# Loading chunk 4's K ahead of three weight pieces, and chunk 2's V beside chunk 3's, in a delta-rule attention and SwiGLU kernel

## The chip, the cores and the metric

The kernel runs on one core of one Trainium2 chip. The metric is the device time of one execution in microseconds; the times given are the median, the lowest and the highest of the runs.

## The reference

The input is `q`, `k`, `v` of shape (4, 8, 768, 48), `beta` of shape (4, 8, 768), all float32, and three weight matrices of a feed-forward block, which arrive as 64-bit floats. An attention without softmax (the delta rule) walks over the 768 positions with one 48 x 48 state for each of the 4 x 8 heads; its output, as 3072 tokens of 384 features, goes through a SwiGLU block:

```python
k_n = k / (np.linalg.norm(k, axis=-1, keepdims=True) + 1e-06)
for t in range(S):
    kt, vt, bt = (k_n[:, :, t], v[:, :, t], beta[:, :, t, None])
    y[:, :, t] = np.einsum('bhd,bhde->bhe', q[:, :, t], state)
    v_old = np.einsum('bhde,bhd->bhe', state, kt)
    state = state + bt[:, :, :, None] * np.einsum('bhd,bhe->bhde', kt, vt - v_old)
x = y.transpose(0, 2, 1, 3).reshape(B * S, H * D)      # (3072, 384)
g = x @ w_gate                                         # (384, 1536)
out = (g * (1.0 / (1.0 + np.exp(-g))) * (x @ w_val)) @ w_out   # w_out (1536, 384)
```

## The kernel before

The 768 positions are cut into 12 chunks of 64. In a chunk the recurrence becomes matrix products: a triangular matrix from the products of K with itself is inverted (for pairs of chunks at once, by substitution), and the state is carried from chunk to chunk. `advance(c)` is a generator that does chunk c's part of the recurrence in steps, so that its small matmuls can be put between the large ones of the feed-forward block of the chunk before. For each chunk, K, Q and V are loaded from DRAM by `load_k(c)`, `load_q(c)` (two DMAs of 192 KB each, in runs of 48 numbers, 192 bytes) and `load_v(c)` (four of 96 KB, in the same runs). `turned(c, of_q)` transposes K or Q on TensorE through the identity (L511), and ScalarE copies the result out of PSUM (L515). K's buffers: chunk 4 uses that of chunk 0 again, and so its load stands in `advance(0)` behind the products that read chunk 0's K last (`of_state`, L1145). V has two buffers, which chunks 2 and 3 take over from chunks 0 and 1.

The weights come in 42 pieces, numbered from 0: 24 of 128 x 256 numbers for features 0 to 1023 (gate and value by turns), 6 of 128 x 512 for the rest, and 12 of the output matrix. A piece is read as it is, two 32-bit words for each weight, into a place that is free at the moment (`stage`, L260: its DMA's queue is SyncE's). ScalarE (`power_step`, L272 and L278) and then VectorE (`convert`, L289, L297, L309) turn the pairs of words into 32-bit weights. The first 23 pieces are staged by hand-written calls. A `stage(n, after)` of these puts a one-element copy on GpSimd ahead of the DMA (L259), which reads a piece `after` that was staged 2 or 3 earlier, and so keeps the DMA back until that piece has landed. The pieces from 23 on are staged by `convert`, when it has freed the place that they take (`freed_by`).

The order on each engine is the order of the program: the whole body stands under a manual schedule. All the loads named here are issued by SyncE, one after the other; a load that waits holds up what stands behind it on that queue, and of the DMAs that it issued at most 8 are on their way at a time, since the ninth takes the semaphore of the first.

The stage around the change is the first 130 us. `chain(at)` runs inside the first two feed-forward groups (chunk 0, f = 0 and 2), four times in each, and advances chunk 0 and then chunk 1 by a step each time. Then follow, for chunks 0 and 1, the groups `(c, f)` in the order (0,4), (0,6), (1,0), (1,2), (1,4), (1,6), (0,8), (1,8), (0,10), (1,10) of `gate_val` (L1409): twelve matmuls each for gate and value, a silu on ScalarE (L1418), a product on VectorE (L1420), and conversions of the next pieces in between (`fill`). Gate and value products go through four PSUM banks by turns, so a group uses the banks of the group two before it. Between groups, `point(2)` puts in a step of preparation: first `turned(4, False)` with `turned(2, True)`, which need K(4) and Q(2), then their products (L527); later the same for K(5). `small_unread(40)`, which stands ahead of `turned(4, False)`, issues tiny matmuls (L658). Behind all groups follow the output products of chunks 0 and 1 (L1436), with the preparation of chunk 2 between them, and from chunk 2 on another form of the feed-forward block (L1313, L1519).

As the kernel stands, the queue of SyncE in this stretch is: pieces 18 to 22, Q(2), V(2), K(4), piece 23, piece 29, V(3), piece 24, K(5), pieces 25, 26, 28, 27.

Of the kernel before, what the change touches and what calls it, by code (L numbers as in the profile page):

```python
# [20 lines left out]
def kernel(  # L21
# [75 lines left out]
    QB = 2  # L97
# [37 lines left out]
    def halves(x, c, b):  # L135
        return x[NB * b : NB * b + NB, :, c * C : (c + 1) * C, :]

    def load_heads(t, x, c, dmas=(nc.sync,)):
        for b in range(2):
            dmas[b % len(dmas)].dma_start(  # L140
                out=t[64 * b : 64 * b + 64, :, :, 0:D].rearrange(
                    "p bp h d -> p (bp h) d"
                ),
                in_=halves(x, c, b).rearrange("bp h p d -> p (bp h) d"),
            )

    def load_k(c, dmas=(nc.sync,)):
        load_heads(kn_of(c), k, c, dmas)

    def load_q(c):  # L150
        load_heads(qpad[c % QB], q, c)
# [28 lines left out]
    def load_v(c):  # L180
        vin[c] = work.tile([128, 2, NB, NJ, D], FP32, name="vin", bufs=2)
        for b in range(2):
            src = halves(v, c, b).rearrange("bp (j par) p d -> par p (bp j) d", par=2)
            for par in range(2):
                s = 64 * (b ^ par)
                nc.sync.dma_start(
                    out=vin[c][s : s + 64, par].rearrange("p bp j d -> p (bp j) d"),
                    in_=src[par],
                )
# [22 lines left out]
    def words(tile_):  # L212
        return tile_.bitcast(U32)
# [32 lines left out]
    def stage(n, after=None, queue=nc.sync):  # L246
        _, src, t, f0, m = pieces[n]
        name, lo = place_of[n]
        if name not in places:
            if name == "p_sb":  # L250
                places[name] = words(p_places[0])
            else:
                places[name] = work.tile(
                    [128, 2 * PIECE], U32, name="staged", tag=name, bufs=1
                )
        place = places[name][:, lo : lo + 2 * m]
        staged[n] = place
        if after is not None:
            nc.gpsimd.tensor_copy(place[:, 0:1], staged[after][:, 0:1])  # L259
        queue.dma_start(  # L260
            out=place, in_=src[t * 128 : (t + 1) * 128, f0 : f0 + m].bitcast(U32)
        )
# [104 lines left out]
    def new_n(g):  # L367

        n_t[g] = work.tile([128, 2, HH], FP32, name="n_t")
# [58 lines left out]
    def load_beta():  # L428
        for s_ in range(2):
            for par in range(2):  # L430
                at = beta_rows(s_).start + 8 * par
                nc.gpsimd.dma_start(
                    out=beta_s[at : at + 8],
                    in_=beta.rearrange(
                        "(b bp) (j par) s -> b par (bp j) s", b=2, par=2
                    )[s_ ^ par, par],
                )
# [123 lines left out]
    def gram(*args):  # L561
        for _ in gram_steps(*args):
            pass
# [384 lines left out]
    def advance(c):  # L948
# [170 lines left out]
                    if n + par < 3:  # L1119
                        yield MORE  # L1120
        if c + 2 < NCH:
            if c < 2:
                load_v(c + 2)
            else:
                late_loads.append(lambda: load_v(c + 2))
        yield
        pq = p_sb.pop(c)
# [489 lines left out]
    def converts(n):  # L1617
        if todo:
            convert(todo[:n])
            del todo[:n]  # L1620
# [9 lines left out]
    def step(kind, fn, *args):  # L1630
        key = (kind, args or (1,))
        if key not in gens:
            gens[key] = [fn(*args), 0]
        if next(gens[key][0], None) != MORE:
            gens[key][1] += 1

    def steps(kind, *args):
        return gens.get((kind, args), (None, 0))[1]
# [123 lines left out]
    with tc.manual_schedule(  # L1762
        engines={
            mybir.EngineType.PE,
            mybir.EngineType.Activation,
            mybir.EngineType.DVE,
            mybir.EngineType.SP,
            mybir.EngineType.Pool,
        }
    ):  # L1770
        new_n(0)
        load_beta()
        first_tiles()
        norms(0)
        norms(1)
        load_q(0)
        load_k(2)
        load_k(3)
        load_q(1)
        load_v(0)  # L1780
        copy_a = nc.scalar.copy
        small_unread(48)
        unread(2)
        turned(0, False, 0)
        p_g = [first_gram(0, "px")]
        turned(1, False, 2)
        first_diag(0, p_g[0])
        spread_beta(copy_a)
        p_g.append(first_gram(1, 2))
        r_b = first_n()  # L1790
        first_diag(1, p_g[1])
        nc.vector.transpose(first_of["mb"][:, 0 : R * R], first_of["flat"])
        first_scale(r_b)
        for n in range(12):
            stage(n, n - 2 if n > 1 else None)
            if n == 9:
                load_v(1)
        stage(12, 10)
        stage(13, 11)
        unread(2, "py")  # L1800
        small_unread(16, "py")
        low_copies(0, p_g[0])
        turned(0, True, 0)
        low_copies(1, p_g[1])
        turned(2, False, "py")
        turned(3, False, "px")
        first_q = [gram_steps(0, True, 2)]
        next(first_q[0])
        turned(1, True, 0)
        gram(2, False, "py", (copy_a, copy_a))  # L1810
        gram(3, False, "px", (copy_a, copy_a))
        unread(2, 0)
        first_q.append(gram_steps(1, True, 0))
        next(first_q[1])
        power_step(0)
        first_substitution()
        for n in range(14, 18):
            stage(n, n - 3)
        first_z()
        some, others = slice(0, HH // 2), slice(HH // 2, HH)  # L1820
        spread_z(0, 1, nc.scalar, some)
        for n in range(18, 23):
            stage(n, n - 3)
        load_q(QB)
        spread_z(0, 0, nc.vector)
        spread_z(0, 1, nc.vector, others)
        scale_v(0)
        next(first_q[0])
        new_nt(0, qpad[1].rearrange("p bp h d -> p (bp h d)"))
        zb_1 = work.tile([128, R, R], FP32, name="zb", bufs=1)  # L1830
        new_nt(1, zb_1.rearrange("p k i -> p (k i)"))
        step("advance", advance, 0)
        next(first_q[1])
        for x in range(2):
            spread_z(1, x, nc.scalar)
        for n in (2, 4, 1, 3, 5, 6, 7):
            power_step(n)
        for _ in range(6):
            step("advance", advance, 0)
        converts_first(0)  # L1840
        step("advance", advance, 0)
        converts_first(2)
        p_n = banks("p_n", "px")
        n_products(1, p_n, (0,))
        step("advance", advance, 0)
        converts_first(4)
        n_products(1, p_n, (1,))
        converts_first(1, 3)
        converts_first(5)
        scale_v(1)  # L1850
        n_copies_1(p_n, zb_1.rearrange("p k i -> p (k i)"))

        def chain(at):

            step("advance", advance, 0 if steps("advance", 0) < 4 else 1)
            converts((1, 2, 2, 1)[at])

        pairs = [(c, f) for c in range(2) for f in range(0, 8, 2)]
        pairs += [(c, f) for f in range(8, FT, 2) for c in range(2)]
        for at, (c, f) in enumerate(pairs):  # L1860
            early = c == 0 and f < 4
            if c == 1 and f == 0:
                finish(1)
                second_inverse.append(invert(1))
                for _ in range(3):
                    next(second_inverse[0])
            elif not early:
                point(2)
            need((6, 12, 18, 24, 30, 30)[f // 2])
            gate_val(c, f, fill, at, chain if early else None)  # L1870
        need(len(pieces))
        for bp in range(NB):
            point(2)
            output(0, bp, fill, (4, 8))
        output(1, 0, fill, (4, 8))
        hold.clear()
        first_blocks(True)
        first_blocks(False)
        point(2)
        output(1, 1, fill, range(2, FT, 2))  # L1880
        finish(2)
        x_sums(2)
        sums_of_w(12)
        for c in range(2, NCH):
            if c > FAST:
                begin(c, 0)
            point(c + 1)
            if c == FAST:
                begin(c, 0)
            for r in range(ROUNDS):  # L1890
                gate_val_fast(c, r, fill)
            output_fast(c, fill)
            finish(c + 1)
            x_sums(c + 1)
# [30 lines left out]
```

## Time and profile before

| | |
|---|---|
| median of 3 runs | 693.07 us (692.01 to 694.98) |
| profiled execution: time | 694.12 us |
| profiled execution: span from first to last instruction | 692.4 us |
| TensorE busy | 675.3 us, 98% |
| VectorE, ScalarE, GpSimd busy | 414.2, 262.9, 193.1 us |
| mean granted clock of TensorE | 0.995 |
| read from and written to DRAM | 53.58 MB, 7.08 MB |

In the lines of the profile PE is TensorE's matmuls, PEld its weight loads, DVE VectorE, ACT ScalarE, POOL GpSimd and SPq the queue of SyncE, from which DMAs are issued. L511 is line 511 of the kernel. A row of a timeline has the start in us, the length in us, the engine, the line, the operation, what is written from what, and how many; in brackets stands the idle time of the engine before it and what ended that. Tiles are named without their numbers, so `kn` is K of any chunk, `zt`, `wo_sb`, `p_sb` and `staged` are places in which pieces are staged, and `ffn` is any of the four banks.

### The profile page before, as it was taken

Reading aid. Unit: us, or ns where it says so; the run is one execution under the profiler, and the core shown is the slowest. Engines: PE = TensorE matmul, PEld = TensorE weight load, DVE = VectorE, ACT = ScalarE, POOL = GpSimd, SP = SyncE. Lnnn points to the kernel's source line nnn. Section 1 sums busy time; section 2 is a strip of 40 time slices with the busy share of each in tenths; the row PEclk is TensorE's granted clock in tenths of the full one; section 3 lists DMA queues with packets and bytes.
Section 4 is the critical chain, followed back from the end, with each engine's and each line's share of the span. In section 5 each row is a group of like instructions: output and inputs, shape, how many; then the busy total and the mean of one; then the engine's idle time right before and its main releaser. Section 6 shows DMA issues by size and latency. Waiting matters only on the chain.

```text
span 692.4 us, 24603 instructions
## 1 busy us (share of the span) xinstructions
PE 675.3 (98%) x10836; PEld 630.0 (91%) x10836; DVE 414.2 (60%) x874; ACT 262.9 (38%) x557; POOL 193.1 (28%) x310
## 2 busy tenths in 40 slices
PE   8897999999999999999999999999999999999997
PEld 4786888756999999999999999999999999999997
DVE  7898489798666765647456546655555534433342
ACT  4785576213543533344323245232143242142230
POOL 5110031105893037820037830208810000000000
PEclk9999899999999999999999999999999999999999
DMA  9667925007561621464333364243243221221210
GB/s 133 160 177 180 257 69 161 1 24 163 134 121 25 114 81 40 97 113 93 78 87 71 70 128 81 55 97 83 55 109 69 56 63 47 55 62 46 70 46 24
DMA packets 143850, 62.24 MB, mean 90 GB/s; under 512 B 122976, under 2 KB 126048, under 8 KB 143744
## 3 DMA queue, kind: packets, MB, share of 16 engines
q1 hardware_dynamic: 141536, 60.19, 37.6%
q8 instruction: 85, 1.39, 0.9%
q10 hardware_dynamic: 2080, 0.39, 0.4%
q14 instruction: 21, 0.17, 0.1%
q0 software_dynamic: 128, 0.10, 0.1%
HBM read 53.58 MB, written 7.08 MB: 88 GB/s over the span
## 4 chain that ended last, share of the span: by engine, by line
PE 91%; DVE 3%; ACT 2%; DMA 2%; issue 1%; SPq 0%; DVEq 0%; ACTq 0%
PE ffn L1313 42%; PE ffn L1519 20%; PE ffn L1409 9%; PE ffn L1436 4%; DMA kn<-in_k_dram 2%; PE p_px L977 2%; PE p_py L960 2%; PE p_px L1043 2%; PE p_py L1133 2%; PE p_px L1145 1%; PE p_px L527 1%; PE p_py L1206 1%; PE ffn L1072 1%; PE p_px L921 1%; PE p_py L935 1%
## 5 line engine op out<-in xcount | busy, mean ns | idle before, releaser
L1313 PE MATMUL ffn<-x_ffn,wg_sb 128*128 128x128 f32 x840 | 128.5, 276 | 0.5 <-ACT ffn L1369 0.3
L1313 PE MATMUL ffn<-x_ffn,wv_sb 128*128 128x128 f32 x840 | 128.2, 275 | 0.0
L1313 PEld LDWEIGHTS ffn<-x_ffn,wg_sb 128*128 128x128 f32 x840 | 111.1, 192 | 1.0 <-ACT ffn L1369 0.7
L1313 PEld LDWEIGHTS ffn<-x_ffn,wv_sb 128*128 128x128 f32 x840 | 110.7, 192 | 0.0
L1348 DVE TENSOR_TENSOR h_f<-sil,ffn 128x256 f32<-128x256 f32 x120 | 49.7, 418 | 83.2 <-ACT sil L1343 81.8
L1343 ACT ACTIVATE sil<-ffn 128x256 f32<-128x256 f32 x120 | 45.8, 383 | 128.5 <-PE ffn L1313 126.4
L1519 PE MATMUL ffn<-wo_sb,h_f 128*128 128x192 f32 x480 | 83.4, 328 | 0.0
L860 POOL TENSOR_TENSOR n_b<-mb,half 128x32 f32<-128x32 f32 x5 | 30.0, 6006 | 183.6 <-DVE mb L569 183.6
L1519 PEld LDWEIGHTS ffn<-wo_sb,h_f 128*128 128x128 f32 x480 | 78.1, 190 | 0.3
L599 POOL TENSOR_TENSOR tmp<-zb,mb 128x31 f32<-128x31 f32 (+15 forms) x124 | 68.6, 553 | 16.9 <-DVE mb L586 7.5
L605 POOL TENSOR_TENSOR zb<-zb,tmp 128x31 f32<-128x31 f32 (+15 forms) x124 | 70.0, 565 | 9.7
L1480 DVE TENSOR_TENSOR ffn<-ffn,p_sb 128x512 f32<-128x512 f32 x58 | 40.4, 696 | 49.1 <-ACT ffn L1369 47.7
L1313 PE MATMUL ffn<-x_t,h_f 128*128 128x128 f32 x480 | 61.0, 280 | 0.2 <-ACT ffn L1326 0.2
L1313 PEld LDWEIGHTS ffn<-x_t,h_f 128*128 128x128 f32 x480 | 56.3, 192 | 2.1 <-ACT ffn L1326 0.3
L1480 DVE TENSOR_TENSOR o_sb<-o_sb,ffn 128x192 f32<-128x192 f32 x49 | 17.2, 352 | 64.1 <-PE ffn L1519 61.5
L1326 ACT COPY ffn<-ffn 128x512 f32<-128x512 f32 x30 | 17.1, 571 | 60.8 <-PE ffn L1313 60.8
L1477 DVE TENSOR_TENSOR h_f<-h_f,h_f 128x256 f32<-128x256 f32 x60 | 29.4, 493 | 11.8 <-PE ffn L1519 10.5
L1519 PE MATMUL ffn<-last_k,h_f 128*128 128x192 f32 x200 | 36.0, 327 | 0.0
L1409 PE MATMUL ffn<-x_ffn,wg_sb 128*128 128x256 f32 x144 | 34.4, 385 | 0.3 <-DVE x_ffn L1210 0.3
L1409 PE MATMUL ffn<-x_ffn,wv_sb 128*128 128x256 f32 x144 | 33.8, 382 | 0.0
L1519 PEld LDWEIGHTS ffn<-last_k,h_f 128*128 128x128 f32 x200 | 32.9, 190 | 0.1
L1409 PEld LDWEIGHTS ffn<-x_ffn,wg_sb 128*128 128x128 f32 x144 | 26.7, 191 | 4.6 <-DVE wg_sb L309 0.8
(323 smaller groups left out, 1123.9 us busy)
## 6 DMA issues: line engine op xcount, KB each, us to landing
h_f<-w_s SPq DMA_DIRECT2D x60, 256.0 KB, 2.8
p_sb<-w_s SPq DMA_DIRECT2D x27, 256.0 KB, 2.8
vin<-in_v_dram SPq DMA_DIRECT2D x48, 96.0 KB, 3.4
out_dram<-o_sb SPq DMA_DIRECT2D x48, 96.0 KB, 2.2
kn<-in_k_dram SPq DMA_DIRECT2D x20, 192.0 KB, 4.6
zt<-in_moe_w_out_dram SPq DMA_DIRECT2D x6, 384.0 KB, 3.9
qpad<-in_q_dram SPq DMA_DIRECT2D x36, 64.0 KB, 3.3
w_s<-h_f SPq DMA_DIRECT2D x7, 256.0 KB, 3.5
```

The lines of the kernel that those rows point to most:

```text
L599: engine.tensor_tensor(out=t_v, in0=zb[:, 0 : j + 1, j : j + 1].to_broadcast([128, j + 1, m]), in1=mb[:, j : j + 1, j + 1 : R].to_broadcas ...
L605: engine.tensor_tensor(out=zb[:, 0 : j + 1, j + 1 : R], in0=zb[:, 0 : j + 1, j + 1 : R], in1=t_v, op=ALU.add,)
L860: nc.gpsimd.tensor_tensor(out=n, in0=mb.rearrange("p j i -> p (j i)")[:, 0 : R * R : R + 1], in1=half, op=ALU.pow,)
L1313: nc.tensor.matmul(p[:, u], w(u), moving, start=start and u == 0, stop=True, skip_group_check=True,)
L1326: nc.scalar.copy(p_y, p_x)
L1343: nc.scalar.activation(sil[:, n].rearrange("p (i n) -> p i n", i=2), p[:, 0:2], ACTF.Silu)
L1348: nc.vector.tensor_tensor(out=h_of(c, f, j), in0=sil[:, n].rearrange("p (i n) -> p i n", i=2), in1=p[:, 2:4], op=ALU.mult,)
L1409: nc.tensor.matmul(ps[name][:, i], w_sb[:, t, (f + i) * 128 : (f + i + 1) * 128], xts[c][:, t], start=(t == 0 and i == 0), stop=(t == KT - 1),
L1436: nc.tensor.matmul(p_o, hs[c, f - f % 2][:, f % 2, bp * 128 : (bp + 1) * 128], wo_sb[:, f], start=(f == 0), stop=(f == FT - 1),)
L1477: nc.vector.tensor_tensor(out=out, in0=a, in1=b, op=ALU.subtract)
L1480: nc.vector.tensor_tensor(out=out, in0=a, in1=b, op=ALU.add)
L1519: nc.tensor.matmul(p[x, part], a(f - f % 2)[:, f % 2], b(f), start=not begun and f == 0, stop=f == FH - 1, skip_group_check=True,)
```

## The change

`load_v(2)`, which stood at the end of `advance(0)`'s correction steps, moves into `advance(1)`, directly ahead of `load_v(3)`. Of the hand-staged pieces, 20, 21 and 22 and then `load_q(2)` move from ahead of the first products of chunk 0 into `chain`, behind the step of chunk 0 that issues `load_k(4)`. SyncE's queue thereby becomes: pieces 18, 19, K(4), pieces 20, 21, 22, Q(2), piece 23, piece 29, V(2), V(3), piece 24, K(5), pieces 25, 26, 28, 27. The instructions of TensorE, VectorE, ScalarE and GpSimd and their order stay as they are; only the semaphores that some of them wait on are other ones.

```diff
         if c + 2 < NCH:
-            if c < 2:
-                load_v(c + 2)
-            else:
+            if c == 1:
+                load_v(2)
+                load_v(3)
+            elif c > 1:
                 late_loads.append(lambda: load_v(c + 2))
...
-        for n in range(18, 23):
+        for n in range(18, 20):
             stage(n, n - 3)
-        load_q(QB)
         spread_z(0, 0, nc.vector)
...
+        later_pieces = list(range(20, 23))
+
         def chain(at):
 
             step("advance", advance, 0 if steps("advance", 0) < 4 else 1)
+            if later_pieces:
+                for n in later_pieces:
+                    stage(n, n - 3)
+                later_pieces.clear()
+                load_q(QB)
             converts((1, 2, 2, 1)[at])
```

## The prediction

> **What bounds the kernel now.** I read the chain of waits first, because TensorE is busy for nearly the whole span and only the chain says where the rest sits. In order of time (start us, length us, what), around the changed place:
>
> ```profile
> 64.18 6.36 DMA kn<-in_k_dram
> ...
> 70.67 1.94 PE p_px L511 x8
> 72.62 1.64 PE p_py L511 x8
> 74.25 5.18 PE ffn L1409 x24
> ...
> 82.56 35.66 PE ffn L1409 x164
> 118.23 0.87 PE p_px L511 x8
> ```
>
> From 55 us to 124 us the chain is TensorE, except for one 6.36 us piece: the load of chunk 4's K, which `turned(4, False)` (L511) transposes. The timeline of TensorE gives the idle time itself, and the windows of 52 to 76 us (us; PE, PEld, DVE, ACT, POOL busy; granted clock; DMA share; GB/s) give clock and transfers:
>
> ```profile
> 65.00 0.70 PE L658 MATMUL p_px<-half 32*32 32x1 f32 x64 [0.19 <-issue]
> 70.67 1.94 PE L511 MATMUL p_px<-ident,kn 128*128 128x128 f32 x8 [4.97 <-DMA kn<-in_k_dram]
> ```
> ```profile
> 52.00:58.00 6.00, 6.00 (x200) 4.90 (x194) 4.22 (x9) 3.88 (x11) 0.68 (x5) 1.00 0.50 163
> 58.00:64.00 6.00, 5.87 (x199) 4.82 (x192) 5.50 (x15) 3.40 (x9) 0.00 (x0) 1.00 0.88 184
> ...
> 66.00:68.00 2.00, 0.00 (x0) 0.00 (x0) 1.90 (x7) 0.00 (x0) 0.00 (x0) 0.81 0.79 179
> 68.00:74.00 6.00, 3.33 (x16) 3.36 (x17) 0.81 (x3) 1.83 (x4) 0.00 (x0) 0.50 0.79 176
> ...
> 80.00:82.00 2.00, 2.00 (x103) 1.88 (x96) 2.00 (x8) 1.46 (x3) 0.00 (x0) 1.00 1.00 406
> ```
>
> So the stall costs twice. TensorE stands from 65.70 to 70.67 us, **4.97 us**, and the granted clock falls to 0.50, so the 16 transposes behind it take 1.94 + 1.64 = 3.58 us. Eight of them take 0.87 us at full clock (118.23), so 2 x 0.87 = 1.74 us would do: another **1.84 us**. Together **6.81 us**. The transfer engines were only half busy from 52 to 58 us, before K was issued.
>
> **Part 1: K(4) goes ahead of pieces 20 to 22.** SyncE's queue as it is now, and the marker copy on GpSimd that releases piece 21:
>
> ```profile
> 52.47 0.38 SPq L260 DMA_DIRECT2D wo_sb<-in_moe_w_val_dram  x1
> 52.94 0.38 SPq L260 DMA_DIRECT2D zt<-in_moe_w_gate_dram  x1
> 56.19 0.33 SPq L260 DMA_DIRECT2D zt<-in_moe_w_val_dram  x1
> 56.83 1.34 SPq L260 DMA_DIRECT2D zt<-in_moe_w_gate_dram  x1
> 58.25 1.32 SPq L140 DMA_DIRECT2D qpad<-in_q_dram  x2
> 59.68 2.97 SPq L186 DMA_DIRECT2D vin<-in_v_dram  x4
> 62.77 2.24 SPq L140 DMA_DIRECT2D kn<-in_k_dram  x2
> 65.13 0.64 SPq L260 DMA_DIRECT2D zt<-in_moe_w_val_dram  x1
> ...
> 66.64 3.69 SPq L186 DMA_DIRECT2D vin<-in_v_dram  x4
> ...
> 74.95 1.63 SPq L260 DMA_DIRECT2D wo_sb<-in_moe_w_val_dram  x1
> ```
> ```profile
> 55.98 0.18 POOL L259 COPY zt<-wo_sb 128x1 uint32<-128x1 uint32 x1 [3.35 <-DMA wo_sb<-in_moe_w_gate_dram]
> ```
>
> Rows for K's issues (ns min/median/max) and its landing, then Q's landing, then V's issues:
>
> ```profile
> L140 SPq DMA_DIRECT2D kn<-in_k_dram x4: 596/748/1370, 62.8 to 74.2; - x4
> ...
> DMA to landing us min/median/max: 4.2/4.8/6.4
> ```
> ```profile
> DMA to landing us min/median/max: 3.8/4.8/5.7
> ```
> ```profile
> L186 SPq DMA_DIRECT2D vin<-in_v_dram x12: 606/633/1505, 36.2 to 69.7; - x12
> ```
>
> Piece 19 is issued at 52.47, 20 at 52.94. In the new program order K's two issues stand between them. K's buffer is free by then: its last readers, chunk 0's 64 L1145 matmuls, stand much earlier in the program. At worst its issues take 1.37 us each, so the second starts at 54.3 and lands 6.4 us later, at 60.7; at best 53.6 + 4.2 = 57.8. TensorE asks at 65.70, so at least 5.0 us of room remain, and the 4.97 us go.
>
> What K pushes: piece 20 from 52.94 to between 54.1 and 55.7. Piece 21 waits for GpSimd's copy (55.98), which waits for piece 18's landing, and piece 18 stays ahead of K, so 21 and 22 keep 56.19 and 56.83. The three copies keep their order on GpSimd, where nothing stands between them and the earlier ones. Cost: nothing, covered by SyncE's 2.87 us of waiting between 53.32 and 56.19; without that cover it would be K's 2.24 us on everything behind.
>
> **Part 2: what is late next.** Q(2) stays at about 58.25, its second half starting near 58.9; 5.7 us later is 64.6. The L511 transposes of it are reached at 65.70 + 0.87 = 66.57, so 2 us remain. Piece 23 no longer stands behind V(2) and K(4). That matters, for ScalarE's rows are:
>
> ```profile
> 71.74 0.43 ACT L272 ACTIVATE wv_sb<-zt 128x256 f32<-128x256 f32 x1 [5.95 <-DMA zt<-in_moe_w_val_dram]
> ...
> 80.54 0.71 ACT L272 ACTIVATE wv_sb<-wo_sb 128x512 f32<-128x512 f32 x1 [1.94 <-DMA wo_sb<-in_moe_w_val_dram]
> ...
> 88.49 3.94 ACT L856 COPY a_sb<-a_sb 32x1024 f32<-32x1024 f32 x2
> ```
>
> ScalarE is in order: today it waits for piece 23 until 71.74, with the copies of K's transposes behind that. Behind Q(2) piece 23 is issued near 59.6, 5.5 us earlier, and so is there near 66.2, 0.4 us after ScalarE begins to wait for it (71.74 - 5.95 = 65.79); the copies behind it are needed by matmuls that come after the next 5.18 us group (74.25), so that costs nothing. V(2) and V(3) aren't urgent: `scale_v(2)` and `advance(2)` stand behind the output of chunks 0 and 1.
>
> **Part 3: the weights behind V.** Here most of the gain could be lost. TensorE comes 6.81 us earlier, but piece 25 (74.95 issue, 80.54 on ScalarE) comes earlier only by what the queue sheds. Everything from 58.25 to 74.95 stays in the stretch, except K's issues: from 62.77 to 65.13, **2.36 us**. V(2) and V(3) keep their eight issues (2.97 + 3.69 us). Bounds: 0 if the transfers rather than the issues set the time and half-used time was not gained, 2.36 if the rows carry over. I take 2.36, since SyncE issued nearly without a break in this stretch.
>
> From 80.54 ScalarE works through its list nearly without a gap to the end of L856 at 92.43, which VectorE waits for. The consequences meet TensorE at the value matmuls of chunk 1, f = 4, whose bank VectorE must have read:
>
> ```profile
> 92.46 2.25 DVE L569 STREAM_TRANSPOSE mb<-a_sb 128x512 f32<-128x512 f32 x2 [2.73 <-ACT a_sb L856]
> ...
> 96.36 0.68 DVE L1420 TENSOR_TENSOR h_f<-sil,ffn 128x512 f32<-128x512 f32 x1
> ```
> ```profile
> 99.93 2.75 PE L1409 MATMUL ffn<-x_ffn,wv_sb 128*128 128x256 f32 x12
> ```
> ```profile
> 130.86 0.69 DVE L1420 TENSOR_TENSOR last_h<-sil,ffn 128x512 f32<-128x512 f32 x1 [3.09 <-PE ffn L1409]
> ```
>
> VectorE is done with that bank at 96.36 + 0.68 = 97.04; TensorE comes at 99.93: slack 2.89 us. TensorE 6.81 us earlier and VectorE 2.36 us earlier leaves a new wait of 6.81 - 2.36 - 2.89 = **1.56 us**. Later VectorE waits 3.09 us for TensorE (130.86), more than the 2.89 us by which it can now trail; from there both go on together, so nothing more is lost.
>
> **Sum.** 6.81 - 1.56 = **5.25 us**. The profiled execution's span of 692.4 becomes 687.2 us, its time of 694.12 us becomes 688.9; the median of the runs shown is 1.05 us lower, 693.07, and 5.25 off that is **687.8 us**.
>
> [...]
>
> **The rivals.**
>
> *All of the lead is kept.* If SyncE sheds more than K's issues (the transfers used the idle half of 52 to 58 us as well, or V's issues get shorter with less ahead of them), the wait at L1409 vanishes: 6.81 us, **686.3 us**. For it: SyncE's 3.69 us for four V issues against 4 x 0.63 = 2.5 us at the median. Against: 3.9 us must be shed.
>
> *The queue sheds little.* If bytes set the time, K's two halves of 192 KB at the 406 GB/s of the 80 to 82 us window are 0.97 us: gain 0.97 + 2.89 = 3.86 us, **689.2 us**; with nothing shed, 2.89 us and 690.2. Against: 163 to 184 GB/s in the stretch, far from 406. [...]
>
> *The new wait drops the clock.* The window of 66 to 68 us has a mean clock of 0.81, so 0.76 us at half: it fell at 67.24, 1.54 us after TensorE's last matmul. A wait of 1.56 us is as long. Then 1.84 us go again: gain 3.41, **689.7 us**. Against: ahead of the old drop stood more than a microsecond of tiny 32x1 matmuls, ahead of the new wait full ones. [...]
>
> *The change doesn't do what it says.* Q(2) becomes the late one and replaces K's wait; to undo all it would have to land 6 us later than now, near 70.5: **693.1 us**.
>
> *Slower: eight V issues in a row hold the weights back.* If each takes the longest row, 1.505 us, the two V loads take 12.04 instead of 6.66 us, and piece 25 comes 5.38 - 2.36 = 3.02 us later than now. The wait at L1409 is then 6.81 + 3.02 - 2.89 = 6.94 us and halves the clock: 6.81 - 6.94 - 1.84 = -1.97, **695.0 us**. It decides once ScalarE gets piece 25 later than 81.6 us (1.05 us later than now). For it: V's issues did stretch behind K. Against: the loads ahead of them are the same ones less K.
>
> **How the numbers follow.** Forecast 0.58, all the lead kept 0.14, little shed 0.10, clock drop 0.08, Q late 0.05, slower 0.05. A measurement of this kernel can tell 0.5%, 3.5 us, from no change. Faster by more: forecast, all kept, 0.06 of little shed, 0.04 of the clock drop, 0.82. Slower by more: 0.03, where the V loads hold more than priced. The rest, 0.15, is within. The range runs from 685.5 (all kept, less 0.8 us, about half of what the shown runs lie off their median: 692.01 and 694.98 against 693.07) to 691.0 (nothing shed, 690.2, and the same allowance), and leaves out the last two cases.
>
> **What would show it.** Right: no idle time before L511 near 66 us, clock 1.00 throughout 64 to 76 us; K issued near 53 us; ScalarE no longer idle 5.95 us before piece 23; piece 25 on ScalarE near 78.2 us; a wait of about 1.5 us before L1409 near 93 us on `ffn`, released by VectorE's L1420; the stretch from there on unchanged. Wrong: a wait of several us before either L511 group; half clock behind the new wait; SyncE's V issues together over 8 us; new idle time after 130 us.

## The result, and the profile after

The changed kernel takes **691.73 us** in the median of 21 runs (689.46 to 693.27), against 693.38 us for the kernel before (21 runs, 691.11 to 695.66). The ratio is 0.9965 (95% interval 0.9954 to 0.9975); it is estimated from the runs and is not the quotient of the two medians. That is 2.4 us gained, between 1.7 and 3.2. The forecast was 687.8 us, 5.25 us less than before. The stall is gone, and over half of what it was to bring did not arrive.

In the timeline of TensorE in the changed kernel (start us, length us, engine, line, operation, count, and in brackets the idle time before and what ended it), the transposes of K stand without a wait:

```profile
67.35 1.09 PE L511 MATMUL p_px<-ident,kn 128*128 128x128 f32 x8
68.28 1.04 PE L511 MATMUL p_py<-ident,qpad 128*128 128x128 f32 x8
...
79.02 1.99 PE L1410 MATMUL ffn<-x_ffn,wg_sb 128*128 128x256 f32 x8 [1.43 <-DVE wg_sb L309]
...
96.96 2.86 PE L1410 MATMUL ffn<-x_ffn,wv_sb 128*128 128x256 f32 x12 [0.41 <-DVE h_f L1421]
...
111.36 2.86 PE L1410 MATMUL ffn<-x_ffn,wg_sb 128*128 128x256 f32 x12 [1.18 <-ACT sil L1419]
```

The windows of the same stretch as before (the figure ahead of the last two is the granted clock) show full clock where it had been 0.81 and 0.50 before:

```profile
66.00:68.00 2.00, 2.00 (x91) 1.78 (x90) 1.78 (x5) 2.00 (x6) 0.00 (x0) 1.00 0.98 296
68.00:74.00 6.00, 6.00 (x36) 5.43 (x34) 2.71 (x9) 3.08 (x7) 0.00 (x0) 1.00 0.70 124
```

What replaced the stall are the three waits below it, 3.02 us together. SyncE's queue in the changed kernel shows why (and, in the second block, piece 24 in the kernel before):

```profile
54.53 0.38 SPq L260 DMA_DIRECT2D wo_sb<-in_moe_w_val_dram  x1
55.01 1.57 SPq L140 DMA_DIRECT2D kn<-in_k_dram  x2
...
59.27 2.08 SPq L140 DMA_DIRECT2D qpad<-in_q_dram  x2
61.46 2.37 SPq L260 DMA_DIRECT2D zt<-in_moe_w_val_dram  x1
63.88 0.44 SPq L260 DMA_DIRECT2D p_sb<-in_moe_w_val_dram  x1
64.37 7.33 SPq L186 DMA_DIRECT2D vin<-in_v_dram  x8
71.81 0.56 SPq L260 DMA_DIRECT2D wo_sb<-in_moe_w_gate_dram  x1
72.47 1.32 SPq L140 DMA_DIRECT2D kn<-in_k_dram  x2
73.89 3.00 SPq L260 DMA_DIRECT2D wo_sb<-in_moe_w_val_dram  x1
```
```profile
70.44 3.00 SPq L260 DMA_DIRECT2D wo_sb<-in_moe_w_gate_dram  x1
```

From the end of Q(2)'s issues to piece 24 it was 10.87 us before (59.57 to 70.44); now it is 71.81 - 61.35 = 10.46. K's issues have left this stretch, but piece 23 takes 2.37 us instead of 0.64 to issue, and the V loads 7.33 instead of 6.66. So ScalarE gets piece 25 no earlier than the 80.54 us of before:

```profile
77.30 0.66 ACT L272 ACTIVATE wg_sb<-wo_sb 128x512 f32<-128x512 f32 x1 [4.75 <-DMA wo_sb<-in_moe_w_gate_dram]
80.66 0.67 ACT L272 ACTIVATE wv_sb<-wo_sb 128x512 f32<-128x512 f32 x1 [2.15 <-DMA wo_sb<-in_moe_w_val_dram]
```

The chain of waits of the changed kernel now runs through this queue and ScalarE's list, where before it was TensorE:

```profile
71.81 0.56 SPq L260
...
73.89 6.74 DMA wo_sb<-in_moe_w_val_dram
80.66 0.67 ACT wv_sb L272
...
90.36 1.95 ACT a_sb L856
92.34 2.25 DVE mb L569 x2
...
111.36 5.45 PE ffn L1410 x24
```

### The profile page after: what moved, and what is told of

It is laid out like the page before. It is cut to its first block, busy times and chain, and to the rows that moved or that the text cites. A ratio compares the mean times of both kernels' runs of the same rounds, so it can differ in the third digit from the quotient of the medians.

```text
span 690.4 us, 24601 instructions
## 1 busy us (share of the span) xinstructions
PE 675.4 (98%) x10836; PEld 629.7 (91%) x10836; DVE 414.0 (60%) x874; ACT 262.6 (38%) x557; POOL 194.3 (28%) x310
## 4 chain that ended last, share of the span: by engine, by line
PE 82%; DMA 8%; ACT 3%; SPq 3%; DVE 2%; issue 1%; POOL 0%; POOLq 0%; DVEq 0%; ACTq 0%
PE ffn L1314 42%; PE ffn L1520 20%; PE ffn L1437 4%; DMA h_f<-in_moe_w_val_dram 2%; PE ffn L1410 2%; PE p_px L977 2%; PE p_py L960 2%; DMA wo_sb<-in_moe_w_val_dram 2%; SPq L140 1%; PE p_py L1134 1%; PE p_px L1043 1%; PE p_px L1146 1%; PE p_px L527 1%; PE p_py L1207 1%; DMA wo_sb<-in_moe_w_gate_dram 1%
## 5 line engine op out<-in xcount | busy, mean ns | idle before, releaser
L605 POOL TENSOR_TENSOR zb<-zb,tmp 128x31 f32<-128x31 f32 (+15 forms) x124 | 72.6, 586 | 9.7
L599 POOL TENSOR_TENSOR tmp<-zb,mb 128x31 f32<-128x31 f32 (+15 forms) x124 | 67.0, 540 | 16.9 <-DVE mb L586 7.4
L1481 DVE TENSOR_TENSOR ffn<-ffn,p_sb 128x512 f32<-128x512 f32 x58 | 40.4, 696 | 48.7 <-ACT ffn L1370 47.3
L1410 PE MATMUL ffn<-x_ffn,wg_sb 128*128 128x256 f32 x144 | 34.5, 385 | 2.9 <-DVE wg_sb L309 1.4
```

The costliest lines, as they stand in the source:

```text
L599: engine.tensor_tensor(out=t_v, in0=zb[:, 0 : j + 1, j : j + 1].to_broadcast([128, j + 1, m]), in1=mb[:, j : j + 1, j + 1 : R].to_broadcas ...
L605: engine.tensor_tensor(out=zb[:, 0 : j + 1, j + 1 : R], in0=zb[:, 0 : j + 1, j + 1 : R], in1=t_v, op=ALU.add,)
L1410: nc.tensor.matmul(ps[name][:, i], w_sb[:, t, (f + i) * 128 : (f + i + 1) * 128], xts[c][:, t], start=(t == 0 and i == 0), stop=(t == KT - 1),
L1481: nc.vector.tensor_tensor(out=out, in0=a, in1=b, op=ALU.add)
```

## The experiments

Three theories. **A**: the weights' path decides; the eight V loads ahead of piece 24 keep it where it was, and so the lead that TensorE gains is spent in new waits. **B**: the new wait near 79 us comes from the place that piece 24 shares with earlier pieces' additions, and is the loss. **C**: the wait for K in the profile of before was a long one, and an ordinary run had less to gain.

**The halves of the change.** K's half alone (V(2) stays in `advance(0)`), and V's half alone (pieces 20 to 22 and Q(2) stay ahead of K). Both cuts are shown against the changed kernel:

```diff
-            if c == 1:
-                load_v(2)
-                load_v(3)
-            elif c > 1:
+            if c < 2:
+                load_v(c + 2)
+            else:
```


> The K half alone: V(2) stays in chunk 0's steps, so that SyncE issues pieces 18, 19, V(2), K(4), 20, 21, 22, Q(2), 23, 29, V(3), 24. Theory A (the eight V issues ahead of piece 24 give the gain back): only four V issues stand ahead of piece 24, the other four use the time in which SyncE waits for GpSimd's copies; piece 24 is issued 2.5 to 4 us earlier than in the changed kernel (71.8 us there), K(4) still lands ahead of 65.7 us, and the waits of TensorE at f = 6 of chunk 0 and later shrink: 688 to 690 us, 2 to 3 us below the changed kernel. Theory B (the wait on piece 24's place holds TensorE, whatever V does): about 691. Theory C (the gain was never more than the stall of 2 us in most runs, the profiled stall of before was a bad one): as the changed kernel, 691.7.

```diff
-        for n in range(18, 20):
+        for n in range(18, 23):
             stage(n, n - 3)
+        load_q(QB)
...
-        later_pieces = list(range(20, 23))
...
-            if later_pieces:
-                for n in later_pieces:
-                    stage(n, n - 3)
-                later_pieces.clear()
-                load_q(QB)
```


> The V half alone: V(2) moves beside V(3), pieces 20 to 22 and Q(2) stay ahead of K(4). Theory A: K(4) is issued about 3 us earlier (near 59.7 instead of 62.8), the stall of 4.97 us shrinks to about 2 us and the clock may stay up; piece 25 comes no earlier than before, so TensorE keeps at most the 2.9 us of slack: 690.5 to 692. Theory C: 693, no change.

K's half: 690.16 us, ratio 0.9959 (0.994 to 0.9979). V's half: 691.53 us, 0.9975 (0.9953 to 0.9996). Each half brings about what the whole does, so they aren't added. K's half came out at the upper end of the 688 to 690 us that theory A expected. In its profile piece 24 is issued 2.57 us earlier than in the changed kernel, as expected, and no wait of TensorE over 0.2 us is left from the transposes of K to 135 us. There is a new one ahead of them, since ScalarE waits 3.81 us for piece 20, which now stands behind V(2) and K(4):

```profile
64.87 0.87 PE L1206 MATMUL p_py<-ident,y 128*128 128x128 f32 x6 [1.38 <-ACT y L1192]
```
```profile
69.24 0.95 SPq L260 DMA_DIRECT2D wo_sb<-in_moe_w_gate_dram  x1
```

That profiled execution, 689.00 us, was the fastest of the twelve. V's half takes V(2) out from ahead of K(4). In its one profile the stall is short, though the kernel before has short stalls too (below): TensorE in V's half waits

```profile
67.06 1.06 PE L511 MATMUL p_px<-ident,kn 128*128 128x128 f32 x8 [0.96 <-DMA kn<-in_k_dram]
```

and then, like the whole change, at later groups (1.61, 0.91, 1.13 and 0.99 us), with piece 25 on ScalarE at 82.42.

**V behind the weights**: V(2) and V(3) are loaded only ahead of group (1,0), behind pieces 24 to 28.

```diff
-            if c == 1:
-                load_v(2)
-                load_v(3)
-            elif c > 1:
+            if c > 1:
...
+                load_v(2)          # ahead of group (1,0)
+                load_v(3)
```


> The changed kernel with V(2) and V(3) issued only ahead of group (1,0), behind pieces 24 to 28, 30 and 31. Theory A: SyncE issues piece 24 near 64.5 instead of 71.8, piece 25 near 67 instead of 73.9; ScalarE no longer waits for them (4.75 and 2.15 us now), the three waits of TensorE (1.43, 0.41 and 1.18 us) go, and the whole 6.8 us lead is kept: 686.5 to 688 us. Theory C: as the changed kernel, 691.7, since the stall of before was not worth 6.8 us in most runs.

**688.15 us**, ratio 0.9926 (0.9901 to 0.9951): 5.1 us less than before, from the same K loads and the same bytes, and 0.15 us above what theory A expected at most. No wait of TensorE over 0.2 us is left from 60 to 135 us. ScalarE gets piece 25 7.5 us earlier than in the changed kernel:

```profile
73.17 0.69 ACT L272 ACTIVATE wv_sb<-wo_sb 128x512 f32<-128x512 f32 x1 [0.85 <-DMA wo_sb<-in_moe_w_val_dram]
```

Theory A holds: what stood in the way was the V loads ahead of the weights.

**Another place for piece 24's powers**: the changed kernel with the order of the places of low words turned.

```diff
-        power = words(hp[10 + (n // 2 % 4 if n < N_HALF else (0, 2, 3, 1)[(n + 2) % 4])])
+        power = words(hp[10 + (n // 2 % 4 if n < N_HALF else (3, 2, 0, 1)[(n + 2) % 4])])
```


> The changed kernel with the low words of pieces 24 and later put into other places in turn ((3, 2, 0, 1) for (0, 2, 3, 1)), so that the additions of pieces 22 and 23 don't wait for ScalarE's step of piece 24. Theory A: the wait of 1.43 us before the gate group of f = 6 goes, but the wait at the value group of chunk 1, f = 4 grows by the same, since it hangs on piece 25 and what ScalarE does behind it: 691.7, unchanged within 0.5 us. Theory B: the wait was what held TensorE: 1.4 us or more below the changed kernel, 690 us.

691.38 us, 0.9964 (0.9947 to 0.9981): the same as the change. The wait near 79 us is gone. Two of the others have grown, to 0.59 and 1.12 us, and the last is 0.22 instead of 1.18 us:

```profile
93.11 2.86 PE L1410 MATMUL ffn<-x_ffn,wg_sb 128*128 128x256 f32 x12 [0.59 <-ACT sil L1419]
97.09 2.86 PE L1410 MATMUL ffn<-x_ffn,wv_sb 128*128 128x256 f32 x12 [1.12 <-DVE h_f L1421]
...
110.53 2.86 PE L1410 MATMUL ffn<-x_ffn,wg_sb 128*128 128x256 f32 x12 [0.22 <-ACT sil L1419]
```

Theory B had expected 690 us, 1.4 us or more below the changed kernel. The best estimate is no gain, and 1.4 us lies at the edge of what the two intervals allow, so theory B is unlikely rather than excluded. The path is late as a whole, and in part the wait that was removed turns up at the next groups that it feeds: 1.93 us in all here, against 3.02.

**The kernel before, profiled again.**

> The kernel before once more, for a second profile of it. If the stall for K(4) and its half clock are a fixed part of the kernel, TensorE again waits 4 to 6 us before L511 and loses 1 to 2 us to the clock; if the first profile was a bad one (theory C), the stall is 1 to 3 us. The first L1007 group, which no change touches, shows how far the time up to there moves from run to run (46.02 in the first profile, 46.1 to 48.1 in the others).

691.46 us, and no wait for K at all, less than either expectation. In this second profile TensorE comes to the first L1007 group at 49.27 us instead of 46.02; in its windows the clock between 20 and 40 us is 0.83. With the 0.50 of the first profile's stall that is 20 x 0.17 / 0.5 = 6.8 us at half clock, an estimate, ahead of everything the change touches:

```profile
68.95 1.09 PE L511 MATMUL p_px<-ident,kn 128*128 128x128 f32 x8
```
```profile
20.00:40.00 20.00, 17.62 (x559) 15.24 (x552) 13.53 (x33) 14.18 (x32) 2.59 (x10) 0.83 0.61 159
```

This is for theory C, and two more profiles of the kernel before follow below.

**The kernel before with V behind the weights**, K as it was:

> The kernel before with V(2) and V(3) issued ahead of group (1,0), and nothing else: pieces 20 to 22 and Q(2) stay ahead of K(4), which then is issued behind Q(2) near 59.7. Theory A: the V loads were the burden on both sides: K(4) lands near 65 to 67, the stall shrinks to 0 to 1.5 us with the clock up, and pieces 24 and 25 come 7 us earlier, so nothing is given back: 688 to 689.5 us, nearly as without V ahead and K first (688.2). If K's place were what matters, it would stay near 691.

690.38 us, 0.9959 (0.994 to 0.9978), above the 688 to 689.5 us that theory A expected. TensorE still waits 1.37 us for K:

```profile
67.79 1.06 PE L511 MATMUL p_px<-ident,kn 128*128 128x128 f32 x8 [1.37 <-DMA kn<-in_k_dram]
```

Taking V out from ahead of the weights without moving K gives 2.8 us, moving K without that gives 2.4 to 2.8, both give 5.1.

**V's issues on GpSimd**: the changed kernel, with V(2) and V(3) issued from GpSimd's queue.

```diff
-                nc.sync.dma_start(
+                (nc.gpsimd if c in (2, 3) else nc.sync).dma_start(
```


> The changed kernel with V(2) and V(3) issued by GpSimd instead of SyncE, at the same place of the program: the same bytes move at the same time or earlier, but SyncE's queue goes from piece 29 straight to piece 24. If the issue on SyncE is the cost (7.33 us), pieces 24 and 25 come about 7 us earlier and the time is near that with V late, 688 to 689; if the transfers themselves are, pieces 24 and 25 are issued early but land late, and it stays at 690.5 to 692.

692.41 us, 1.0001 (0.998 to 1.0021): the whole gain is gone, which lies above both times expected. GpSimd issues the eight in 5.70 us from 58.44, and SyncE reaches piece 24 at 64.36 instead of 71.81. But K(5)'s two issues then take 5.03 us, ScalarE waits 4.18 us for piece 23, and TensorE stands 2.42 us ahead of K's transposes, which run in part at a lower clock (0.72 in the mean from 68 to 74 us):

```profile
68.31 0.70 PE L658 MATMUL p_px<-half 32*32 32x1 f32 x64 [2.42 <-issue]
68.95 1.46 PE L511 MATMUL p_px<-ident,kn 128*128 128x128 f32 x8
```
```profile
71.06 0.43 ACT L272 ACTIVATE wv_sb<-zt 128x256 f32<-128x256 f32 x1 [4.18 <-DMA zt<-in_moe_w_val_dram]
```

Here V's transfers also start 6 us earlier, beside those of Q and piece 23. So freeing SyncE of the issues doesn't help while V moves ahead of the weights; that the transfers themselves are the price is consistent with this but not isolated by it, and what ended the 2.42 us the profile doesn't say.

**The clock kept up**: the kernel before, with five more matmuls that nobody reads ahead of `turned(4, False)`.

```diff
+            unread(WARM)     # WARM = 5
```


> The kernel before with five full 128x32x512 matmuls (about 0.87 us each) ahead of turned(4), so that TensorE works through the wait for K(4) instead of idling: only the clock's part of the stall is taken away. Expected of the 1.84 us: 1.0 to 1.9 us below the kernel before, 691.5 to 692.4, since that little lead fits into the 2.9 us of slack behind it. If the half clock cost nothing, 693.4.

692.91 us, 0.9992 (0.9972 to 1.0013). The clock stays at 1.00 through the wait for K, which the added matmuls fill down to 1.08 us, and the transposes run at full speed:

```profile
66.15 4.50 PE L651 MATMUL p_px<-half 128*32 128x512 f32 x10
71.73 1.06 PE L511 MATMUL p_px<-ident,kn 128*128 128x128 f32 x8 [1.08 <-DMA kn<-in_k_dram]
```

The best estimate is a gain of 0.6 us, with 1.84 us near the edge of the interval (1.9). This doesn't isolate the clock: the added matmuls take 4.50 us, and where the wait for K is shorter than that (0, 2.51 and 2.69 us in the other profiles of the kernel before) they hold K's transposes up themselves. In this run K and piece 25 (83.17 on ScalarE) were late as well.

**Three more profiles**, two of the kernel before and one of the changed kernel, and **K(5) behind the weights too**:

> The kernel before, profiled once more. Theory C (the wait for K with its half clock is no fixed cost of the kernel before; it depends on where short stretches of half clock ahead of it and the transfers put TensorE and K in a run): the wait before L511 may be anything from 0 to 5 us, and the profiled span differs from 692.4 us by less than 2 us whatever it is. Theory A (the wait is there in each run and its 6.8 us are given back behind it): 4 to 6 us of wait, and the absence in the earlier look was the exception.

> The same as for the third look: theory C, a wait between 0 and 5 us that doesn't set the span; theory A, 4 to 6 us of wait.

> The changed kernel, profiled once more. Both theories: no wait before L511 near 66 us. Theory A: SyncE's eight V issues together over 6.5 us again, piece 24's issue 10 to 11 us behind the end of Q(2)'s issues, piece 25 on ScalarE within 0.5 us of 80.6. Rival (the queue sheds 2.36 us in an ordinary run, and the first look was a bad one): piece 24's issue 8.5 us behind the end of Q(2)'s, piece 25 near 78.2, and a span near 687.

```diff
                 load_v(2)          # ahead of group (1,0)
                 load_v(3)
+                load_k(5)
```


> The changed kernel with V(2), V(3) and K(5) all loaded behind the weights, ahead of group (1,0). In the version with V alone moved there no wait of TensorE over 0.2 us was left from 60 to 135 us. If the weights' path sets the time only through TensorE's waits, taking 1.9 us more off the queue ahead of piece 25 gains nothing: 688.1 us, within 0.5 of the version with V alone moved. If K(5) comes late at its own transposes (112 us), slower by 1 to 2 us: 689 to 690. If the weights' path still costs something that the waits don't show: 686 to 687.

The two executions of the kernel before took 692.59 and 693.64 us, with waits of

```profile
69.43 1.35 PE L511 MATMUL p_px<-ident,kn 128*128 128x128 f32 x8 [2.51 <-DMA kn<-in_k_dram]
```
```profile
69.99 1.53 PE L511 MATMUL p_px<-ident,kn 128*128 128x128 f32 x8 [2.69 <-DMA kn<-in_k_dram]
```

Theory A had expected 4 to 6 us of wait in each, theory C anything from 0 to 5 us with a span within 2 us of 692.4. The second profile, with 689.8 us, lies 2.6 us off, these two within 1.5. The changed kernel took 691.86 us in its second profile. There the V loads took 8.21 us, and piece 24 stood 71.94 - 61.41 = 10.53 us behind Q(2)'s issues, as theory A expected. Piece 25 came to ScalarE at 81.96 us, later than expected (80.6):

```profile
59.09 2.32 SPq L140 DMA_DIRECT2D qpad<-in_q_dram  x2
...
63.62 8.21 SPq L186 DMA_DIRECT2D vin<-in_v_dram  x8
71.94 0.56 SPq L260 DMA_DIRECT2D wo_sb<-in_moe_w_gate_dram  x1
```
```profile
79.11 1.99 PE L1410 MATMUL ffn<-x_ffn,wg_sb 128*128 128x256 f32 x8 [1.52 <-DVE wg_sb L309]
...
94.28 2.86 PE L1410 MATMUL ffn<-x_ffn,wg_sb 128*128 128x256 f32 x12 [0.23 <-ACT sil L1419]
98.24 2.86 PE L1410 MATMUL ffn<-x_ffn,wv_sb 128*128 128x256 f32 x12 [1.11 <-DVE h_f L1421]
```

With K(5) late too: **687.98 us**, 0.993 (0.9903 to 0.9956), the same as with V alone, though piece 25 reaches ScalarE at 71.67, another 1.5 us earlier. Once the weights come early enough, no wait of TensorE over 0.2 us is left from 67 to 135 us in either version, and nothing more is to be had there. Both versions are faster than the kernel before, and by their ratios than the changed kernel.

**The profiles side by side** (us; start of the first L1007 group, the wait for K, the end of Q(2)'s transposes, piece 25 on ScalarE, and the start of K(5)'s transposes):

| kernel, profile | clock 20 to 40 us | L1007 | wait for K | end of Q(2)'s | piece 25 | K(5)'s | span |
|---|---|---|---|---|---|---|---|
| before, 1st | 1.00 | 46.02 | 4.97 | 74.25 | 80.54 | 118.06 | 692.4 |
| before, 2nd | 0.83 | 49.27 | 0 | 70.92 | 78.98 | 115.34 | 689.8 |
| before, 3rd | 0.91 | 47.81 | 2.51 | 72.49 | 80.64 | 116.86 | 690.9 |
| before, 4th | 0.91 | 48.11 | 2.69 | 73.23 | 80.25 | 117.42 | 691.9 |
| after, 1st | 0.91 | 48.07 | 0 | 69.32 | 80.66 | 116.65 | 690.4 |
| after, 2nd | 0.91 | 47.76 | 0 | 69.32 | 81.96 | 116.93 | 690.1 |
| V late | 1.00 | 46.60 | 0 | 67.99 | 73.17 | 111.81 | 686.3 |
| V and K(5) late | 1.00 | 45.84 | 0 | 67.43 | 71.67 | 111.24 | 686.0 |

From K(5)'s transposes to the end of the span it is 573.2 to 574.8 us in each row, so nearly all of the difference lies ahead of that (the rows of after lie 0.9 us below those of before in the mean). From L1007 to the end of Q(2)'s transposes it is 28.23, 21.65, 24.68 and 25.12 us in the four profiles of before, and 21.25 and 21.56 after: the stall with its clock costs 6.8, 0.2, 3.3 and 3.7 us above the 21.4 of after, **3.5 us in the mean**. In the third and fourth 2.51 and 2.69 us of that are waiting, which leaves 0.8 and 1.0 us to the clock (0.84 from 64 to 75 us in both). From the end of Q(2)'s transposes to K(5)'s it is 43.8, 44.4, 44.4 and 44.2 before, 47.3 and 47.6 after, and 43.8 in both late versions: the change pays back **3.3 us**.

## Why the prediction was wrong

*The stall (6.81 us).* As a saving in that one run it was right: in the first profiles the stretch from L1007 to the end of Q(2)'s transposes shrinks by 28.23 - 21.25 = 6.98 us. As the price of an ordinary run it was too large: 3.5 us in the mean of four profiles, from 0.2 to 6.8. The 4.97 us belonged to a run in which no half clock came from 20 to 40 us (1.00), so TensorE arrived earliest; in the profile where it arrived last, 3.25 us later, there was no wait. The third and fourth lie between in both. K's landing moves from run to run too (in the three with a wait it ended at 70.67, 69.43 and 69.99 us), so that the half clock makes the whole spread is argued, not shown. The shown median lay 1 us under the profiled execution, and the prediction took that for an offset without asking whether the profiled stall was a long one. In its sum the stall cancels, however: 6.81 - (6.81 - 2.36 - 2.89) = 2.36 + 2.89. Its size matters only in runs where it is smaller than what the weights' path lets through.

*Part 1, K ahead of the pieces.* Right: K is issued 55.01 to 56.58, between pieces 19 and 20, and TensorE never waits for it. SyncE stood about 2 us later in this run from piece 18 on (54.11 against 52.04), before anything that was moved.

*Part 2, what is late next.* Q(2) and piece 23 were in time as said; ScalarE takes piece 23 at 67.66 without a wait. What was missed: with its wait for piece 23 gone, ScalarE waits 4.75 us for **piece 24** instead, and VectorE's additions for earlier pieces wait behind that:

```profile
78.54 0.42 DVE L309 CUSTOM_DVE_ANT_0 wg_sb<-wg_sb,last_h 128x512 uint16<-128x512 uint16 x1 [1.29 <-ACT last_h L278]
```

This gives the 1.43 us of TensorE near 79 us, which no step of the prediction had.

*Part 3, the queue behind V.* This is the step that failed. It took the queue to shed K's 2.36 us in full; between the first profiles it shed 0.41 us. From the end of Q(2)'s issues to piece 24 the other three profiles of the kernel before have 11.56, 10.91 and 10.80 us, and the second of the changed kernel 10.53, so it is 0.5 us between the means. The text named the condition ("0 if the transfers rather than the issues set the time") and then took the other end, because SyncE issued without a break. With K's issues gone, piece 23's and V's rows grew by 1.73 and 0.67 us, 2.40 together. The eight semaphores didn't hold these rows: the load eight places earlier had landed before the row began (for the first V load at 60.96 us, and its row starts at 64.37). From 60 to 80 us the DMA engines were 0.91 to 0.97 busy in the four profiles of before, and 0.94 in the two of after. That fits rows stretched by what is still moving, but what holds a row is argued, not shown.

So piece 25 came at 80.66 and 81.96 us, not at 78.2. Counted from the first L1007 group it comes after 32.6 and 34.2 us, against 34.5, 29.7, 32.8 and 32.1 us before, so it is not earlier in that count either. With 0.41 in place of 2.36 the sum's new wait is 6.81 - 0.41 - 2.89 = 3.51 us, and the stretch from Q(2)'s transposes to K(5)'s grew by 47.33 - 43.81 = 3.52 us between the first profiles. The waits seen in it add up to 3.02 us, and to 3.04 in the second (1.52, 0.23, 1.11 and, near 111 us, 0.18), instead of 1.56. The wait foreseen at the value matmuls of group (1,4), released by L1421, is there (0.41 and 1.11 us), one of three or four.

*The sum.* With 0.41 us shed it gives 2.89 + 0.41 = 3.30 us, so this term makes up 1.95 of the 2.85 us by which the forecast missed 2.4. The other 0.9 us fit runs with a smaller slack or stall than the first profile. The slack is the time from the end of VectorE's L1420 to TensorE's value matmuls of group (1,4). In the second to fourth profiles of before it is 1.32, 1.78 and 2.69 us (95.28 to 96.60, 96.95 to 98.73, 96.59 to 99.28). If a run gains its slack and 0.41 us, but no more than its stall, the four give 3.3, 0.2, 2.2 and 3.1 us, 2.2 in the mean. That is an estimate from four profiles.

*The clock behind the new wait.* Right: no drop, 1.00 from 60 to 120 us in both profiles, with waits of at most 1.43 and 1.52 us.

*The rivals.* "The queue sheds little" was what happened, and "eight V issues in a row" was its mechanism in part: the eight took 7.33 to 8.21 us and piece 25 went past its deciding point, 81.6 us, in one of two profiles. The kernel was still not slower there, as the waits stayed near 3 us. With nothing shed the queue rival's gain is the slack, 2.89 us, inside the measured 1.7 to 3.2; the time that it named, 690.2 us, lies 1.5 us below the median of the runs. The second half of the forecast, that TensorE's lead stays once the weights keep up, is what the version with V behind the weights shows: 688.15 us.

*What stays open.* The profiles give 3.5 - 3.3 = 0.2 us at K(5)'s transposes and 1.0 us between the mean spans (691.25 and 690.25), the runs 1.7 to 3.2 us. Four profiles and two are few for a stall that varies by 5 us. The version with V behind the weights has no stall and pays nothing back in its profile, and its runs gain 5.1 us (3.4 to 6.9); that points to a mean stall above 3.5 us, but the interval includes both. Where the 0.9 us behind K(5) come from isn't settled either.

## What to carry to other kernels

Before pricing a stall, see whether it has its size in a second profile: a wait between two paths that drift against each other isn't a constant, and where the other path lies close behind, no more is gained than the slack of that path and what it gets faster. When a load is moved ahead on a queue, ask what stays between it and the weights that decide the next stretch: here putting the loads nobody is waiting for behind the weights was worth as much as removing the stall. And a wait that is removed on a late path, like the place of piece 24, can turn up at the next groups.

## What the runs showed of the hardware

Short stretches of half clock come at places that differ from run to run: in the windows from 20 to 40 us four profiles of the same kernel had mean clocks of 1.00, 0.83, 0.91 and 0.91, by estimate 0, 6.8, 3.6 and 3.6 us at half. In windows of 1 us the first profile of the changed kernel has 0.51, 0.50, 0.50 and 0.78 from 33 to 37 us, which is 3.4 us at half; the first one of the kernel before has 0.61 from 67 to 68 us and 0.50 from 68 to 74, which is 6.8 us, in and behind the stall. TensorE came to the first L1007 group 3.25 us later in the profile with 6.8 us at half from 20 to 40 us than in the one with none. If work at half clock takes twice as long (eight transposes took 1.64 us at 0.50 and 0.87 at full clock), 6.8 / 2 = 3.4 us are lost, an estimate. The 3.25 us are more than the change gained.

Eight V loads of 96 KB in runs of 192 bytes held SyncE's queue for 7.33 and 8.21 us in the two profiles of the changed kernel, against 6.59 to 6.89 us for the two groups of four in the four profiles of before. Issued by GpSimd they took 5.70 us, and then K(5)'s two issues on SyncE took 5.03 us instead of 1.32: the loads behind them took longer in its place.
